# A new list of steps for the first stage and the first pair of a fused attention and FFN kernel

## Chip, cores and metric

The kernel runs on one core of one Trainium2 chip. The metric is the device time of one execution in microseconds, of which three runs of the kernel before are given, and one further execution was profiled.

## What is computed

Attention in two directions between x (8 batches, 8 heads, 512 rows, 64) and a state (32 rows), then two feed-forward layers over the 8 x 544 rows of 512 that come out of it:

```python
def _attn_ref(x, state):
    scores = scale * np.matmul(x, state.transpose(0, 1, 3, 2))
    ...
    xread = np.matmul(a, state)
    scores2 = scale * np.matmul(state, x.transpose(0, 1, 3, 2))
    ...
    sread = np.matmul(a2, x)
    return np.concatenate([xread, sread], axis=2)

def _moe_ref(x, w_in, w_out, g_ln):          # w_in 512x1024, w_out 1024x512
    h = x @ w_in
    ...                                      # solu = h * softmax(h), layer norm, times g_ln
    return ln @ w_out

def _moe2_ref(x, w_in, w_out):               # w_in 512x2048, w_out 2048x512
    h = x @ w_in
    g = np.maximum(0.01 * h, h)
    return g @ w_out
```

## The kernel before

The kernel has a first stage, a first pair of the second feed-forward layer, and three more pairs.

**The first stage** runs over eight batches b. Per batch it loads the state (`z`, in four pieces) and x (`xn`, in four pieces), transposes both on TensorE (tiles `zt`, `xt`), takes the scores (`st`), turns them and normalizes them on VectorE (`q`, `ee`), turns the two attention matrices (`a2t` on TensorE; `a1T` on VectorE by STREAM_TRANSPOSE), reads the state (`sr`) and forms state @ w_in (`sw` for the first batches, `sv` later, the latter from tiles `wi` loaded back from a DRAM copy `wsc`). The hidden rows `h` are a matmul of `a1T` with that product; they are normalized on VectorE and ScalarE (`sn`, `e`), turned (`tr` into `ln`) and multiplied by w_out (tiles `x2_b_r`, `x` in the profile), and the result leaves for a DRAM buffer (`xo` to `xs`). The weights arrive as 64-bit numbers (`raw_in`, `raw_out`) and are narrowed to f32 on ScalarE and VectorE first: for each quarter one Abs, two TENSOR_SCALAR and two SCALAR_TENSOR_TENSOR.

**The first pair** is the second feed-forward layer for the first two batches, in eight chunks of its width: the weights are narrowed and split, `hX`/`h` rows (`H`), the leaky step (`C`, `S`, `g`), and the second product (`o` added into `oacc`) which at the end goes out (`out<-oacc`, two transfers of 1 MB). With it run the rows of the states (`out8`, `oacc8`). **The later pairs** use a scheme with seven products (`hX`, `hY`, `hZ`, `oX`, `oY`, `oZ`), written in `rest()` from the lists PATTERN, HEAD and TURN. The first steps of the first later chunk are mixed into the tail of the first pair (tokens that begin with `/8.`).

**What sets the order.** Every operation is a generator that yields after each step. The string PROGRAM names generators; each occurrence of a name runs the next step of that generator:

```python
    for u in PROGRAM.split():
        if u not in stages:
            stages[u] = stage(u)
        if stages[u] is not None:
            next(stages[u], None)
```

The letters: `a` loads a quarter of w_in, `i` narrows it, `j` splits it into two parts, `b`, `o`, `p` the same for w_out; `z` and `x` load state and x of a batch, `Z` and `T` turn them, `S` is the scores, `U` the softmax, `A` and `B` turn the attention matrices, `R` reads the state, `Y` and `W` form state @ w_in, `w` loads a `wi` tile, `h` makes hidden rows, `t` turns them, `X` multiplies by w_out. `D`, `c`, `d`, `H`, `O`, `K`, `Q` are the first pair, `F` is `rest()`.

The class `InOrder` wraps every engine and the SP queue and ties each instruction to the one before it there, so each engine runs what the string says in that order and nothing is rescheduled. Because that helper records every instruction, all have the line L51 in the profile. Buffers are taken from rings when a step takes one and go back when the last user drops it (`take`, `drop`):

```python
    def take(ring, name, uses=1):
        held[name] = [ring, free[ring].pop(0), uses]
        return f"{ring}{held[name][1]}"
```

so the string also decides which buffer each tile lives in and whose release it waits for. All transfers are issued by the SP queue, one after the other.

Of the kernel before, what the change touches and what calls it, by code (L numbers as in the profile page):

```python
# [64 lines left out]
def attn_solu_leaky_kernel(  # L65
# [1291 lines left out]
    a0 i0 i0 i0 i0 i0 z0. Z0.1 a1 x0.0 T0.0 Z0.0 a3 i1 i1 i1 Z0.0 Z0.0 z1. i1 T0.0 i1 T0.1 T0.1  # L1357
    a2 S0.0 x0.1 i3 Z0.1 Z1.1 i2 Z1.1 Z0.1 T0.3 Z1.1 T0.2 Y0.0.0 i3 i3 i3 T0.3 z2. i2 i2 i2 T0.2
    i2 Z1.0 S0.1 Y0.0.0 S0.0 S0.0 Z1.0 Z1.0 j2 j2 b0 i3 S0.1 S0.1 o0 U0.0 U0.1 S0.0 b2 b3 o2
    Y0.0.1 S0.0 U0.0 U0.1 S0.1 S0.1 Y0.1.0 S0.1 S0.0 Y0.0.1 Y1.0.0 U0.1 U0.1 Y0.1.1 U0.1 U0.0  # L1360
    U0.0 U0.0 A0.1 b1 g Y1.0.0 A0.0 Y0.1.0 j3 Y1.1.1 o2 o2 A0.0 A0.1 R0 j2 Y1.1.1 Y0.1.1 B0.0 o0
    o1 Z2.0 B0.1 o1 Y1.1.0 R0 Z2.0 x1 o1 o0 o1 h0.1 Z2.0 Z2.0 h0.1 Y1.1.0 R0 h0.0 o1 o1 o0 R0
    Z2.0 h0.1 Y1.0.1 h0.1 Y1.0.1 o2 T1.0 h0.0 o0 T1.0 h0.1 h0.1 z3. T1.1 T1.1 h0.0 Z2.1 o2 S1.0
    h0.0 T1.2 T1.3 T1.2 S1.0 S1.0 T1.3 h0.0 h0.0 S1.0 S1.1 S1.0 S1.1 S1.1 h0.1 h0.0 U1.1 h0.2
    S1.1 h0.0 o0 h0.3 S1.0 U1.1 Z2.1 U1.0 U1.1 h0.0 h0.3 S1.1 h0.1 S1.1 U1.0 U1.0 h0.1 A1.0 A1.0
    A1.1 A1.1 h0.0 j1 t0.0.0 t0.0.0 U1.1 U1.1 h0.2 h0.1 t0.1.0 h0.3 t0.0.1 U1.0 U1.0 t0.1.0 h0.3
    h0.2 h0.3 j3 t0.0.1 R1 R1 B1.0 Z3.0 B1.1 h0.3 h0.2 h0.2 t0.1.1 h0.2 t0.1.1 h1.2 x2. R1 h0.3
    h0.3 h0.3 Z2.1 Z3.0 Z3.0 h1.2 h0.2 h1.0 R1 h0.3 t0.3.1 Z3.0 Z2.1 Z2.1 Z3.0 h0.2 t0.3.0 T2.2
# [60 lines left out]
    h6.1 h7.1 t6.1.0 t6.2.0 t6.2.0 h7.1 h7.0 t6.3.0 X5.1 X5.3 t6.2.1 h7.1 t6.3.1 h7.0 t6.1.0
# [93 lines left out]
```

## Time and profile before

| | |
|---|---|
| time, three runs | 1155.01, 1156.82, 1158.55 us (median 1156.82) |
| the profiled execution | 1156.16 us, span 1154.4 us |
| instructions | 16468 |
| matmuls | 6192 records, TensorE busy 98% of the span |
| VectorE, ScalarE, GpSimd | busy 78%, 47%, 47% |

In the profile's rows PE is TensorE, PEld its weight loads, DVE VectorE, ACT ScalarE, POOL GpSimd, SP (or SPq) the queue that issues the transfers. An instruction is named by the tile it writes and those it reads, so `xt<-ident,xn` turns a piece of x. Square brackets behind a row hold the idle time of the engine before it and what it waited for. Times are microseconds from the start of the span.

### The profile page before, as it was taken

What the parts mean: (1) busy time and instruction counts of PE and PEld (TensorE: products, weight loads), DVE (VectorE), ACT (ScalarE), POOL (GpSimd) and SP (SyncE); (2) the same over time, 40 slices, a digit from 0 to 9 for tenths busy, and PEclk for the clock granted to TensorE, in tenths of its full rate; (3) what the DMA queues carried; (4) which work ended last, traced back from release to release, by engine and by line L of the source; (5) the groups of instructions that cost most, each with busy time, mean ns of one, the idle gap of its engine ahead of it and who ended that gap; (6) DMA issues with size and microseconds to landing.
All of it is one profiled execution on the core that took longest, in us unless ns stands there. A gap on an engine that the chain in (4) does not pass through costs nothing.

```text
span 1154.4 us, 16468 instructions
## 1 busy us (share of the span) xinstructions
PE 1128.9 (98%) x6192; PEld 945.8 (82%) x6192; DVE 895.7 (78%) x1406; ACT 540.7 (47%) x907; POOL 540.2 (47%) x411
## 2 busy tenths in 40 slices
PE   6999999999999999999999998999999999999997
PEld 2565887888888888888887888998898998899997
DVE  7997868786887678468777977788977868877787
ACT  5676746655655554644343343334442324433231
POOL 2142420111202133756757458878656656745453
PEclk9999999999999999999999999999999999999999
DMA  9333222503523344763755585766877476655342
GB/s 317 93 107 136 55 96 64 139 19 92 152 70 108 130 162 155 246 210 131 243 208 202 183 346 220 289 238 229 318 292 273 179 278 254 236 222 236 148 192 74
DMA packets 88376, 211.85 MB, mean 184 GB/s; under 512 B 41320, under 2 KB 49512, under 8 KB 79080
## 3 DMA queue, kind: packets, MB, share of 16 engines
q1 hardware_dynamic: 88296, 210.79, 51.7%
q8 instruction: 49, 0.80, 0.3%
q14 instruction: 31, 0.25, 0.1%
HBM read 151.00 MB, written 59.77 MB: 183 GB/s over the span
## 4 chain that ended last, share of the span: by engine, by line
PE 89%; DMA 4%; DVE 3%; issue 1%; POOL 1%; ACT 0%; POOLq 0%; SPq 0%; DVEq 0%; ACTq 0%
PE x L51 17%; PE hX L51 14%; PE oX L51 10%; PE h L51 10%; PE o L51 8%; PE hY L51 7%; PE oY L51 5%; PE hZ L51 3%; PE tr L51 3%; PE sr L51 2%; PE oZ L51 2%; PE st L51 2%; PE sv L51 1%; DVE C L51 1%; PE sw L51 1%
## 5 line engine op out<-in xcount | busy, mean ns | idle before, releaser
L51 DVE TENSOR_TENSOR oacc<-oacc,oX 128x512 f32<-128x512 f32 x171 | 116.2, 683 | 52.9 <-PE oX L51 51.0
L51 PE MATMUL x<-ln,w_out_hi 128*128 128x512 f32 (+1 forms) x512 | 153.8, 384 | 0.0
L51 PE MATMUL hX<-xbT,w 128*128 128x512 f32 x576 | 149.9, 395 | 1.5 <-ACT C L51 1.2
L51 ACT COPY C<-hX 128x512 f32<-128x512 f32 x96 | 56.4, 587 | 171.1 <-PE hX L51 171.0
L51 PEld LDWEIGHTS hX<-xbT,w 128*128 128x128 f32 x576 | 103.4, 188 | 21.3 <-ACT C L51 1.6
L51 PEld LDWEIGHTS x<-ln,w_out_hi 128*128 128x128 f32 x512 | 92.2, 188 | 17.6
L51 PE MATMUL h<-sw,a1T 128*128 128x512 f32 x352 | 103.6, 436 | 0.0
L51 PE MATMUL x<-ln,w_out_lo 128*128 128x512 f32 (+1 forms) x256 | 97.2, 380 | 0.0
L51 POOL TENSOR_TENSOR gc<-C,gc 128x512 fp32r<-128x512 f32 (+1 forms) x43 | 69.3, 1614 | 50.2 <-ACT gc L51 25.5
L51 POOL TENSOR_TENSOR gb<-C,gb 128x512 fp32r<-128x512 f32 (+1 forms) x43 | 69.8, 1629 | 45.9 <-ACT gb L51 23.6
L51 DVE SCALAR_TENSOR_TENSOR C<-C 128x512 f32<-128x512 f32 (+1 forms) x88 | 82.7, 940 | 0.6
L51 PEld LDWEIGHTS h<-sw,a1T 128*128 128x128 f32 x352 | 64.1, 188 | 23.2 <-issue 11.0
L51 DVE TENSOR_TENSOR C<-C,hY 128x512 f32<-128x512 f32 x64 | 43.9, 686 | 43.7 <-ACT C L51 35.2
L51 DVE TENSOR_TENSOR oacc<-oacc,oY 128x512 f32<-128x512 f32 x93 | 63.3, 683 | 2.7 <-PE oY L51 2.0
L51 DVE TENSOR_TENSOR oacc<-oacc,o 128x512 f32<-128x512 f32 x70 | 45.7, 681 | 21.6 <-PE o L51 21.3
L51 PEld LDWEIGHTS x<-ln,w_out_lo 128*128 128x128 f32 x256 | 48.1, 188 | 9.8
L51 DVE TENSOR_TENSOR ln<-tr,ln 128x512 fp32r<-128x512 f32 x60 | 40.4, 684 | 17.9 <-ACT ln L51 17.5
L51 POOL TENSOR_TENSOR gb<-S,gb 128x512 fp32r<-128x512 f32 x27 | 44.6, 1656 | 16.8 <-ACT gb L51 8.1
L51 ACT CAST ln<-tr 128x512 fp32r<-128x512 f32 x60 | 34.5, 588 | 35.3 <-PE tr L51 35.2
L51 PE MATMUL hX<-xbB,w 128*128 128x512 f32 x192 | 50.9, 401 | 0.0
L51 POOL TENSOR_TENSOR gc<-S,gc 128x512 fp32r<-128x512 f32 x26 | 39.3, 1521 | 24.6 <-ACT gc L51 12.7
L51 PE MATMUL hY<-xbB,w 128*128 128x512 f32 x192 | 49.7, 394 | 0.4 <-DVE C L51 0.4
(696 smaller groups left out, 2801.8 us busy)
## 6 DMA issues: line engine op xcount, KB each, us to landing
w<-w2s SPq DMA_DIRECT2D x24, 1792.0 KB, 11.6
shared<-wo2s SPq DMA_DIRECT2D x24, 768.0 KB, 4.3
wi<-wsc SPq DMA_DIRECT2D x14, 1024.0 KB, 5.7
xs<-xo SPq DMA_DIRECT2D x34, 256.0 KB, 2.4
raw<-in_moe_w_in SPq DMA_DIRECT2D x8, 1024.0 KB, 5.6
raw<-in_moe_w_out SPq DMA_DIRECT2D x8, 1024.0 KB, 6.3
w2s<-w SPq DMA_DIRECT2D x8, 1024.0 KB, 8.1
wo<-wt2s SPq DMA_DIRECT2D x8, 1024.0 KB, 6.3
```

The costliest lines, as they stand in the source:

```text
L51: done = call(*args, **kw)
```

## The change

The string PROGRAM is written anew: 142 lines become 143, and nearly every token stands elsewhere. No instruction is added, removed or changed; the last token `F`, and so the three later pairs, is the same. What differs is the order on each engine up to the end of the first pair, the order of the transfers on SP up to there, and which buffers the tiles take. The first two lines of the list, the place of the load of x for batch 4, and the last two lines:

```diff
-    a0 i0 i0 i0 i0 i0 z0. Z0.1 a1 x0.0 T0.0 Z0.0 a3 i1 i1 i1 Z0.0 Z0.0 z1. i1 T0.0 i1 T0.1 T0.1
-    a2 S0.0 x0.1 i3 Z0.1 Z1.1 i2 Z1.1 Z0.1 T0.3 Z1.1 T0.2 Y0.0.0 i3 i3 i3 T0.3 z2. i2 i2 i2 T0.2
...
-    Z5.0 R3 t2.3.0 t2.3.1 h3.0 t2.0.0 x4. Z5.0 Z5.0 t2.3.1 t2.3.1 h3.0 t2.0.1 t2.0.0 t2.3.0
...
-    /8.t3 /8.t2 /8.hS3 /8.hS2 Q7.1 O0.7.1.1 /8.gA12 /8.t4 /8.hS4 O0.7.1.3 /8.gS3 /8.gS2 O0.7.1.1
-    O0.7.1.3 /8.ub /8.uc /8.gS1 /8.gS4 /8.gA22 Q7.1 F
+    a0 i0 i0 i0 a1 x0.0 T0.0 z0. i1 T0.0 T0.1 Z0.0 Z0.0 i0 a3 i0 a2 Z0.1 z1. T0.1 i1 i1 Z0.1 i1
+    Z0.1 i1 Z0.0 i3 i3 S0.0 i3 S0.0 i2 S0.0 Y0.0.1 x0.1 Y0.0.1 b0 S0.0 b2 i2 i3 i2 Z1.0 Z1.0
...
+    h2.3 h2.3 h2.3 w2.0 h2.3 t2.0.0 X1.3 X1.2 X1.3 t2.0.0 Z5.0 Z5.0 h3.0 h3.0 Z5.0 t2.3.0 t2.3.0
+    x4. T4.0 T4.0 T4.2 T4.1 h3.3 h3.3 h3.0 t2.3.0 T4.2 T4.2 h3.0 T4.1 T4.0 t2.2.0 h3.0 t2.2.0
...
+    O0.7.1.2 /8.t4 /8.hS2 /8.gS2 /8.hS4 O0.7.1.1 O0.7.1.1 /8.gS1 O0.7.1.3 /8.ub /8.uc /8.gS3
+    /8.gS4 F
```

Three places at which the order moves:

VectorE, about 32 to 42 us, where the first batch's a1T is made (`ee` is the attention matrix, `wo` and `w_out_f` the quarters of w_out, `sm` the softmax sums). Before:

```order
L51 TENSOR_REDUCE sm0_0_295<-ee0_256 128x16
L51 TENSOR_SCALAR sm0_0_295<-sm0_0_295 128x16
L51 RECIPROCAL sm0_0_295<-sm0_0_295 128x16
L51 TENSOR_SCALAR wo2_264<-wo2_264 128x1024 x2
L51 STREAM_TRANSPOSE a1T1_335<-ee0_256 128x512
L51 TENSOR_SCALAR wo0_254<-wo0_254 128x1024
L51 STREAM_TRANSPOSE a1T1_335<-ee0_256 128x512
L51 TENSOR_SCALAR wo1_338<-wo1_338 128x1024 x2
L51 TENSOR_SCALAR wo0_254<-wo0_254 128x1024
L51 SCALAR_TENSOR_TENSOR wo1_338<-raw_out0_246,wo1_338 128x1024
L51 TENSOR_TENSOR stq_87<-zt2_0_340,stq_87 128x64
```

Now:

```order
L51 RECIPROCAL sm0_0_313<-sm0_0_313 128x16
L51 TENSOR_SCALAR wo1_308<-wo1_308 128x1024
L51 TENSOR_REDUCE sm0_1_341<-ee0_272 128x16
L51 TENSOR_SCALAR sm0_1_341<-sm0_1_341 128x16
L51 RECIPROCAL sm0_1_341<-sm0_1_341 128x16
L51 TENSOR_SCALAR wo1_308<-wo1_308 128x1024
L51 TENSOR_TENSOR stq_87<-zt2_1_306,stq_87 128x64
L51 STREAM_TRANSPOSE a1T1_352<-ee0_272 128x512
L51 COPY srT_89<-sr0_318 64x4x32
L51 TENSOR_TENSOR stq_87<-zt2_1_306,stq_87 128x64
L51 SCALAR_TENSOR_TENSOR wo0_250<-raw_out0_211,wo0_250 128x1024
L51 STREAM_TRANSPOSE a1T1_352<-ee0_272 128x512
```

Both halves of `a1T1` now stand behind more of the narrowing of w_out: its last half has three further TENSOR_SCALAR and one SCALAR_TENSOR_TENSOR of `wo` ahead of it. Up to the a1T of the second batch both lists hold the very same instructions of VectorE.

SP, where x of batch 4 is loaded (`wi2_0`, `wi2_1` are 1 MB tiles of split w_in, `xs` are results on their way to DRAM). Before:

```order
L51 DMA xs1_67<-xo1_2_1349 128x512
L51 DMA wi2_0_1357<-wsc0_98 128x2048
L51 DMA wi2_1_1361<-wsc1_99 128x2048
L51 DMA xn_91<-in_x 128x8x64 x4
L51 DMA xs1_67<-xo1_3_1395 128x512
```

Now:

```order
L51 DMA z0_83<-in_state 32x2x64 x4
L51 DMA wi2_0_1400<-wsc0_98 128x2048
L51 DMA xs1_67<-xo1_2_1301 128x512
L51 DMA xn_91<-in_x 128x8x64 x4
L51 DMA wi2_1_1517<-wsc1_99 128x2048
L51 DMA xs1_67<-xo1_3_1411 128x512
```

The load of `wi2_1` moves from just ahead of the four pieces of `xn` to just behind them; a load of the state comes to stand ahead of `wi2_0`.

SP at the end of the first pair (`out` the results, `wf2` the first of the f32 weights that the later pairs take differences of, `wt2s`, `shared` the second product's weights). Before:

```order
L51 DMA w2_1_1_5488<-w2s1_103 128x3584
L51 DMA out_0<-oacc_3932 128x2048
L51 DMA out_0<-oacc8_4157 4x32x512
L51 DMA wt2s0_130<-wo2_1_0_5349 128x2048
L51 DMA shared_5350<-wo2s1_111 128x1536
L51 DMA out_0<-oacc_3932 128x2048
L51 DMA wt2s1_131<-misc_3964 128x2048
L51 DMA out_0<-oacc8_4157 4x32x512
L51 DMA wf2_5596<-wf2s2_120 128x1024
L51 DMA w2_1_2_5613<-w2s2_104 128x3584
```

Now:

```order
L51 DMA w2_1_1_5471<-w2s1_103 128x3584
L51 DMA shared_5351<-wo2s1_111 128x1536
L51 DMA wt2s0_130<-wo2_1_0_5350 128x2048
L51 DMA out_0<-oacc8_4202 4x32x512 x2
L51 DMA out_0<-oacc_3934 128x2048 x2
L51 DMA wt2s1_131<-misc_3930 128x2048
L51 DMA wf2_5596<-wf2s2_120 128x1024
L51 DMA w2_1_2_5613<-w2s2_104 128x3584
```

The two transfers of `oacc`, of 1 MB each, now stand side by side ahead of `wt2s1` and `wf2`, where before the first of them stood at the front; `shared`, `wt2s0` and both `oacc8` now go ahead of them.

## Rows read from the trace of the kernel before

**Rows 1.** Page, part 1: the span, and each engine's busy time, share and instructions.

```profile
span 1154.4 us, 16468 instructions
PE 1128.9 (98%) x6192; PEld 945.8 (82%) x6192; DVE 895.7 (78%) x1406; ACT 540.7 (47%) x907; POOL 540.2 (47%) x411
```

**Rows 2.** TensorE's waits, whole span: us in total, times, longest.

```profile
PE zt L51 <- DMA z<-in_state: 6.9, 1, 6.9
PE xt L51 <- DMA xn<-in_x: 5.3, 5, 2.3
```

**Rows 3.** Busy time by stretch, 0 to 66 us (stretch, its length, busy times).

```profile
0.00:20.00 20.00, 9.29 (x24) 4.49 (x25) 12.14 (x14) 8.36 (x15) 3.87 (x11) 1.00 0.94 276
...
sum 66.00, PE 55.04 PEld 31.28 DVE 56.95 ACT 40.53 POOL 15.73; mean PE 18.35 PEld 10.43 DVE 18.98 ACT 13.51 POOL 5.24
```

**Rows 4.** Busy time by stretches of 50 us: PE first, GB/s last.

```profile
150.00:200.00 50.00, 48.07 (x259) 40.16 (x258) 36.65 (x78) 27.18 (x56) 8.30 (x14) 1.00 0.30 90
200.00:250.00 50.00, 50.00 (x263) 41.93 (x262) 41.43 (x79) 30.83 (x58) 6.92 (x11) 1.00 0.32 88
...
650.00:700.00 50.00, 46.90 (x258) 40.66 (x257) 39.58 (x48) 22.75 (x36) 26.65 (x19) 1.00 0.65 246
```

**Rows 5.** Timeline of TensorE, first 66 us: start, us, operation, [idle before].

```profile
6.92 0.44 PE L51 MATMUL zt<-ident,z 128*128 128x128 f32 x1 [6.92 <-DMA z<-in_state]
9.63 1.99 PE L51 MATMUL xt<-ident,xn 128*128 128x128 f32 x4 [2.27 <-DMA xn<-in_x]
...
29.99 1.04 PE L51 MATMUL a2t<-ident,q 128*128 128x128 f32 x8
...
65.65 1.88 PE L51 MATMUL h<-sw,a1T 128*128 128x512 f32 x4
```

**Rows 6.** Timeline of VectorE, first 66 us.

```profile
7.17 1.42 DVE L51 TENSOR_SCALAR wi<-wi 128x1024 f32<-128x1024 f32 x2 [7.17 <-ACT wi L51]
8.63 1.23 DVE L51 SCALAR_TENSOR_TENSOR wi<-raw_in,wi 128x1024 uint32<-128x1024 uint32 x1
...
64.45 1.30 DVE L51 STREAM_TRANSPOSE a1T<-ee 128x512 f32<-128x512 f32 x2
```

**Rows 7.** Timeline of SP, 165 to 182 us (the duration is that of issuing).

```profile
165.68 0.92 SPq L51 DMA_DIRECT2D wi<-wsc  x2
168.84 7.42 SPq L51 DMA_DIRECT2D xn<-in_x  x4
```

**Rows 8.** Timeline of TensorE at the same place.

```profile
181.15 1.20 PE L51 MATMUL xt<-ident,xn 128*128 128x128 f32 x9 [1.93 <-DMA xn<-in_x]
```

**Rows 9.** Page, part 6: transfers, KB each, median us from issue to landing.

```profile
wi<-wsc SPq DMA_DIRECT2D x14, 1024.0 KB, 5.7
```

**Rows 10.** Timeline of TensorE, 302 to 305 us.

```profile
302.24 1.89 PE L51 MATMUL sr<-ee,xn 128*128 128x64 f32 x16
303.94 0.94 PE L51 MATMUL sv<-wi,stq 128*128 128x512 f32 x3
304.73 1.89 PE L51 MATMUL sr<-ee,xn 128*128 128x64 f32 x16
```

**Rows 11.** The chain that ended last, two of its pieces: start, us, what.

```profile
211.85 4.10 PE x L51 x18
...
306.62 4.19 PE x L51 x18
```

**Rows 12.** Timeline of SP at the end of the first pair.

```profile
678.20 0.34 SPq L51 DMA_DIRECT2D out<-oacc  x1
...
681.78 0.84 SPq L51 DMA_DIRECT2D wf<-wf2s  x1
```

**Rows 13.** Timeline of GpSimd there.

```profile
693.14 0.74 POOL L51 TENSOR_TENSOR wd<-wf 128x256 f32<-128x256 f32 x1 [8.55 <-DMA wf<-wf2s]
```

**Rows 14.** Timeline of TensorE there.

```profile
699.03 0.84 PE L51 MATMUL oX<-shared,gc 128*128 128x256 f32 x4 [3.10 <-POOL gc L51]
```

**Rows 15.** Busy time there, with clock, DMA share and GB/s at the end.

```profile
676.00:695.00 19.00, 19.00 (x123) 17.18 (x122) 12.09 (x16) 9.93 (x18) 10.06 (x8) 1.00 0.97 371
```

More of the change, by code (lines that the diff above doesn't have):

```diff
@@ new lines @@
+    h1.3 o3 h1.1 h1.1 U2.1 U2.1 h1.3 S2.1 p3 o2 S2.1 U2.0 j1 h1.2 W1.0.0 W1.0.1 h1.2 W1.0.0
+    W1.0.1 W1.0.0 W1.0.1 W1.0.0 W1.0.1 h1.0 X0.1 X0.1 h1.0 U2.0 U2.0 W1.1.0 U2.1 W1.1.0 X0.2
+    w1.3 W1.3.1 X0.2 X0.2 U2.0 X0.2 p2 U2.1 W1.3.1 U2.0 S2.0 W1.3.1 h1.0 h1.0 h1.2 h1.2 h1.2
+    h1.3 h1.3 W1.3.1 X0.1 B2.0 X0.1 X0.2 j1 W1.1.0 W1.1.0 X0.0 X0.0 h1.0 t1.0.0 S2.1 X0.0 X0.2
+    h1.3 W1.3.1 B2.0 t1.0.0 B2.0 h1.1 W1.1.0 p0 A2.1 X0.0 A2.1 W1.3.0 h1.3 t1.0.0 X0.0 A2.0
+    t1.0.1 U2.1 B2.1 A2.0 W1.3.0 h1.3 X0.3 h1.1 W1.1.1 X0.3 t1.0.1 t1.0.1 X0.0 X0.3 h1.1 W1.1.1
@@ new lines @@
+    h4.2 h4.2 B5.1 X3.3 B5.1 Z7.0 B5.1 h4.3 h4.3 Z7.0 Z7.0 Z7.0 X3.2 Z7.0 h4.3 X3.3 X3.3 X3.3
+    t4.1.1 h4.2 h4.2 h4.2 X3.2 B5.0 t4.1.1 t4.1.1 B5.0 B5.0 T6.0 R5 X3.2 T6.3 T6.0 T6.0 T6.1
+    T6.3 T6.3 t4.1.0 T6.1 T6.1 h5.0 X3.3 X3.2 t4.1.0 t4.1.0 h5.0 T6.2 h5.0 T6.2 T6.2 t4.3.0
+    t4.3.0 t4.3.1 t4.2.0 h5.1 t4.3.0 h5.0 X3.2 t4.2.1 t4.3.1 h5.0 t4.2.0 h5.0 S6.0 t4.2.0 h5.0
+    S6.0 t4.3.1 S6.0 h5.1 X4.2 S6.1 U6.0 S6.0 h5.1 t4.2.1 Z7.1 S6.0 S6.0 h5.0 t4.2.1 h5.0 h5.0
+    S6.1 S6.1 h5.2 h5.2 S6.1 U6.1 U6.1 X4.2 X4.2 h5.1 h5.1 Z7.1 h5.1 h5.2 w3.1 U6.1 t5.0.0
@@ new lines @@
+    X4.3 B6.0 x7. W3.2.0 W3.3.0 X4.3 W3.3.1 W3.3.0 W3.3.1 W3.2.1 X4.3 W3.2.1 W3.3.1 h6.0 t5.2.0
+    h5.1 t5.2.1 W3.2.1 W3.2.1 t5.2.0 t5.2.0 t5.1.1 h6.0 h6.0 h6.3 t5.2.1 t5.2.1 h6.3 W3.2.1
+    t5.1.0 t5.1.1 t5.1.1 T7.0 h6.0 h6.0 t5.3.0 t5.3.0 T7.1 h6.3 h6.2 T7.1 t5.3.0 h6.2 T7.1
+    t5.1.0 t5.3.1 h6.0 T7.3 t5.1.0 T7.0 T7.0 X5.2 h6.3 h6.3 T7.3 T7.2 X5.2 t5.3.1 t5.3.1 T7.2
+    h6.2 T7.2 S7.0 X5.2 S7.0 S7.0 h6.0 h6.0 T7.3 h6.2 h6.3 S7.1 h6.3 U7.0 S7.1 h6.0 X5.0 X5.0
+    X5.0 X5.0 U7.1 S7.0 h6.2 h6.1 h6.3 h6.2 U7.0 U7.0 h6.0 U7.1 U7.1 S7.1 S7.1 h6.2 S7.0 X4.3
@@ new lines @@
+    d4.0.0 d2.1.2 Q1.1 Q1.1 K2 d4.0.0 d3.0.3 d3.0.3 O0.1.0.2 O0.1.0.2 d4.0.0 H0.2.6 d4.0.0
+    O0.1.0.0 d4.0.1 d4.0.3 d4.0.3 H0.3.1 H0.3.2 H0.3.2 d4.0.3 d4.0.3 H0.2.7 Q1.0 K2 H0.2.6 Q1.0
+    H0.3.3 H0.3.4 O0.1.0.3 O0.1.0.3 H0.2.6 d2.1.1 O0.1.1.0 H0.3.4 H0.3.4 O0.1.1.1 d4.0.2 H0.2.5
+    H0.3.5 O0.0.1.1 O0.1.1.0 d2.1.4 K2 O0.1.1.3 K2 d4.0.2 K3 d5.0.0 H0.3.6 H0.3.1 O0.1.0.0
+    d5.0.0 K3 H0.3.5 H0.3.5 H0.4.0 H0.4.1 d5.0.0 d3.1.0 H0.2.5 d5.0.0 O0.1.1.3 d4.0.3 d4.0.3
+    O0.1.1.2 H0.4.0 H0.4.2 K2 H0.3.6 H0.4.2 O0.2.1.1 d3.0.5 K3 d3.1.0 d3.1.0 H0.3.7 H0.3.5
@@ new lines @@
+    Q3.0 d5.1.0 d4.0.5 H0.5.2 K4 H0.4.7 K4 H0.5.3 d6.0.0 d6.0.0 H0.5.2 H0.5.4 H0.5.4 H0.4.5
+    O0.3.0.1 H0.4.6 d5.1.0 O0.3.0.2 d4.1.2 Q4.1 d5.0.4 d6.0.0 O0.3.1.3 O0.3.0.2 Q3.0 H0.4.5
+    d5.1.0 d6.0.3 H0.5.1 d6.0.2 d6.0.3 d6.0.3 K5 O0.3.1.1 d6.0.2 K5 H0.5.4 H0.5.5 O0.3.0.0
+    H0.5.6 d5.1.0 d5.1.1 d6.0.1 H0.4.6 d5.1.5 O0.4.0.2 d5.0.5 O0.3.1.1 O0.3.0.3 K5 H0.5.5 d6.0.3
+    H0.5.5 O0.4.0.2 d6.0.4 H0.6.0 Q4.1 O0.3.1.2 H0.5.7 O0.3.0.3 O0.3.1.2 d6.0.3 d4.1.4 H0.5.6
+    H0.6.0 H0.5.6 d6.0.3 O0.3.1.0 d5.1.2 H0.6.1 H0.6.2 O0.4.0.3 H0.6.1 H0.6.2 O0.3.1.0 d5.1.2
@@ new lines @@
+    Q5.0 d7.1.0 Q5.0 H0.6.6 H0.6.6 H0.6.5 Q5.1 H0.7.2 H0.7.3 K6 Q5.1 /7.U O0.5.0.2 /7.ua K6
+    d7.1.0 d7.1.0 O0.5.1.3 H0.7.2 H0.7.4 /7.W H0.7.4 H0.7.4 O0.5.0.1 K6 H0.6.5 Q6.0 d7.1.0
+    H0.7.5 H0.7.6 L1.1 Q6.0 O0.5.0.0 H0.7.6 O0.6.0.3 H0.7.7 O0.6.0.3 O0.5.1.1 H0.7.6 d7.1.2
+    d7.1.2 O0.6.1.2 O0.5.1.1 O0.6.1.2 H0.7.5 H0.7.5 O0.5.0.2 O0.6.1.1 d6.1.4 H0.7.5 O0.6.1.1
+    H0.7.5 O0.6.0.2 O0.6.0.1 O0.6.0.2 O0.6.1.0 d7.1.5 O0.6.0.0 O0.5.0.1 k1.1 O0.6.0.1 k1.0 Q6.1
+    O0.6.1.3 /7.V l1 f1.0 k1.0 k1.6 f1.1 d7.0.4 d7.0.5 k1.3 k1.3 O0.6.1.0 f1.3 k1.1 k1.2 /8.m0
```

224 lines of the change are left out of this document (94 added, 130 removed).

## The prediction

> **What bounds the kernel now.** The page's first part comes first: TensorE is busy 1128.9 of 1154.4 us, and no other engine gets beyond 82% [rows 1]. So no step can win more than the 25.5 us in which TensorE stands still, unless its matmuls themselves come closer together. The change ends before about 700 us, so the next question is how much of that idle time lies ahead of it. The table of busy time by stretches answers: 10.71 us in the first 20 us [rows 3], 1.93 between 150 and 200, nothing between 200 and 250 (and so in the other stretches up to 600, within 0.3), 3.10 between 650 and 700 [rows 4]. Some 16 us in all are open to the new list, two thirds of them at the start.
>
> What these are is told by TensorE's waits and its timeline. The first matmul waits 6.92 us for the first load, which no order of steps makes arrive much earlier, since something must be loaded first [rows 2, 5]. Waits for x cost 5.3 us [rows 2]: 2.27 at 9.63 us [rows 5], 1.93 at 181.15 us [rows 8], and the 1.1 left over between them at the start (5.3 - 2.27 - 1.93). The 3.10 us at 699 us are a wait for GpSimd [rows 14].
>
> One more limit does not show in TensorE's own rows. VectorE starts at 7.17 us [rows 6] and is busy 56.95 of the 58.83 us from there to 66.00 [rows 3]. The hidden rows of the second batch, at 65.65 us, start as the last a1T transposes end, at 64.45 + 1.30 us [rows 5, 6]. So up to 66 us VectorE is as much the bound as TensorE; behind that TensorE alone.
>
> **The change part by part.** Nothing is added, so the cost of each part is a wait that goes or comes.
>
> *Start: taken as 0.* The list loads both halves of the first w_in tile first, then x, then the state, and puts two groups of `sw` matmuls ahead of the second half of x. The same bytes are queued in a stretch where the transfers are busy 0.94 of the time [rows 3], so the first products can't come much earlier or later. The two groups can fill the 1.1 us for which TensorE waits for x. What decides is what becomes of it: the second batch's a1T has the very same VectorE instructions ahead of it in both orders (the order's first place shows them swapped, not added), and VectorE had 58.83 - 56.95 = 1.9 us of idle time to lose or give. A lead that TensorE wins before is lost in waiting for that a1T at about 65.7 us. The first batch's a1T comes later than before, by three TENSOR_SCALAR (half of 1.42 each) and one 1.23 us SCALAR_TENSOR_TENSOR [rows 6], 3.4 us, and TensorE waits for it in the hidden rows; but that wait too lies ahead of the same 65.7 us. Ends: -1.1 (the wait for x goes, and VectorE closes as much of its idle time) and +1.9 (VectorE loses as much again as it stood idle before). I take 0, because VectorE's own work is the same and hardly any of its idle time can go.
>
> *x of batch 4: -1.9.* Before, two loads of `wi` (1 MB each) are issued at 165.68 us, right ahead of the four pieces of x, whose issuing then takes 7.42 us [rows 7]; TensorE stands 1.93 us for the last [rows 8]. Now one of the two goes behind x. At the 371 GB/s that the transfers reach when they are saturated [rows 15], 1 MB is 2.8 us, more than the wait. The state's load that now stands ahead is 16 KB a piece by its shape. So the wait goes. Ends: -1.93, and -1.0 if the queue ahead is otherwise fuller.
>
> *A load of wi at about 300 us: +0.4.* In the new list the last `wi` tile of round 3 (`wi3_2`) takes the buffer that `sv3_0_0` frees, and its first use `sv3_2_0` stands behind 16 `sr` matmuls, 3 `sv` and 12 `x` matmuls. From start to start these take 1.70 and 0.79 us [rows 10] and 12 x 0.23 = 2.75 us [rows 11], 5.2 us in all; such a load takes 5.7 us in the median [rows 9]. The rest, 0.5 us, is less where the queue is empty, as it is around 300 us; I take 0.4. Ends: 0, and 1.5 if the store of `xs` (256 KB by its shape) ahead of it on SP is still in flight. The Trainium skill (DMA: Bandwidth & Descriptors, section Bandwidth) lists 6.15 us for a load of 1 MB; by that the term would be 0.9 and the sum 0.5 us higher. The trace's own 5.7 stands here.
>
> *End of the first pair: 0.* Before, `wf` is issued at 681.78 us [rows 12] into a queue that moves 371 GB/s at a share of 0.97 [rows 15]; GpSimd, in order, stands 8.55 us for it until 693.14 us [rows 13] with the `gc` behind it for which TensorE then waits 3.10 us [rows 14]. Now the first `out` (1 MB) is issued beside the second, at about 678 us [rows 12] instead of at the front of this stretch, so 2.8 us of transfer are added right ahead of `wf`; `shared` (0.75 MB by its shape) and one `out<-oacc8` (0.25 MB) go ahead earlier by as much, 2.8 us. The last step of the pair and so the last `out` stays where it is in TensorE's work. These cancel. Ends: -3.1 (the wait is gone) and +2.8 (the 1 MB without what goes ahead).
>
> Everything between has buffers and loads as long ahead as before, as far as the order shows; TensorE is without a gap there [rows 4] and I count 0 for it. Sum: 0 - 1.9 + 0.4 + 0 = -1.5 us against the profiled execution's own 1156.16 us, 1154.7 us. That execution is 0.66 us below the median of the three runs; against the median of 1156.82 the forecast is **1155.3 us**. Its own range is 1153.4 to 1158.5: the terms' nearer ends (start -0.5 to +1.0, x -1.0 to -1.9, wi 0 to 1, end of the pair -1 to +1) and a little more for the runs, which are 3.5 us apart themselves. A measurement of this kernel tells about 0.3%, 3.5 us, from no change, so the forecast is a change that can't be told.
>
> **The rivals.**
>
> *Faster: the waits go.* The start keeps the 1.1 us, x of batch 4 gives 1.9, and the wait for `gc` at 699 us goes wholly (3.1), because `shared` and the small outputs leave the queue early enough that `wf` lands 3 us sooner. 1156.8 - 6.1 = 1150.7 us. For it: all three are waits for transfers, and the list touches the order of all three. Against it: VectorE's limit at 65.7 us, and 1 MB more just ahead of `wf`.
>
> *Slower: the outputs side by side.* The two `out` transfers wait for the pair's last sums, and SP runs in order, so `wt2s1` and `wf` stand behind them now. If VectorE's last sums come 3 us later than before, everything behind them on SP is issued so much later, and 1 MB more lies in the queue (2.8 us): `wf` lands up to 5.8 us later, GpSimd's `wd` and `gc` with it, and the wait of 3.1 becomes 8.9. With the -1.5 of the other terms, 1156.8 - 1.5 + 5.8 = 1161.1 us. It decides from the point at which `wf` lands 1.5 us later than before (no gain left) and is told from no change from 5 us on. For it: GpSimd already stands 8.55 us for this transfer [rows 13], so every microsecond goes through. Against it: 1 MB leaves the stretch as well.
>
> *Slower: VectorE at the start.* If VectorE waits for a load or for TensorE's scores in the first 66 us, each microsecond passes to the end; it had only 1.9 us of idle time. With 5 us of it: 1160.3 us. For it: more of w_out's narrowing stands ahead of the a1T. Against it: the same work, and a start of VectorE that hangs on the same first load.
>
> *The matmuls' own distance.* Two pieces of the chain with the same 18 matmuls take 4.10 and 4.19 us [rows 11], so the distance from matmul to matmul isn't quite constant: 2%. TensorE's rows show no gap for it. A list that gives tiles other buffers could shift a part: 500 matmuls of the touched part, each nearer or farther by those 0.09 / 18 = 0.005 us, are 2.5 us, up or down, within what can't be told. The Trainium skill (Perfetto Trace Analysis, its opening note) calls the busy time of matmuls a bad metric, because they are pipelined, and would read the 82% of the weight loads instead; by that far more than 16 us could be open to an order. No row of before bears it out beyond those 2%, so it gets a small chance.
>
> **How the numbers follow.** The forecast 0.54; faster by the waits 0.20; the outputs 0.14; VectorE at the start 0.06; the matmuls' distance 0.06, half up and half down and mostly within 0.3%. That gives faster by over 0.3% (below 1153.3) 0.23, with a part of the forecast's low edge; within it 0.55; slower (above 1160.3) 0.22. The range of eight in ten takes in the faster rival's 1150.7 and the slower one's 1161.1: 1150.5 to 1161.5.
>
> **What the profile after would show.** Start: TensorE's hidden rows of the second batch at 65.2 to 66.5 us, right behind a1T. If they come at 64 the start gains, at 68 VectorE was the bound. Batch 4: no wait for xn near 180 us, and 5.3 us of such waits down to 3.4 or less. At 300 us: a wait of `sv` for `wi` of up to 1 us. End of the pair: `wf` landing 11 to 12 us after its issue, and a wait of `oX` for `gc` of 2 to 4 us. I am wrong if a wait of more than 2 us shows between 66 and 650 us, if the wait for `gc` is gone or doubled, or if the same matmuls take longer without a gap.

## The result, and the profile after

The new list takes 1145.01 us in the median of four runs (1144.2 to 1146.07), beside 1157.62 us for the one before (four runs, 1155.01 to 1158.55): a ratio of 0.9895, 95% interval 0.9876 to 0.9915, some 12 us or 1% less. The forecast was 1155.3 with a range from 1150.5; the time lies below it. The profiled execution of the new list took 1145.32 us.

Its page, part 1 [rows 1 before], and TensorE's waits [rows 2 before]:

```profile
span 1143.5 us, 16477 instructions
PE 1124.3 (98%) x6192; PEld 944.0 (83%) x6192; DVE 894.3 (78%) x1406; ACT 539.6 (47%) x907; POOL 540.8 (47%) x411
```

```profile
PE xt L51 <- DMA xn<-in_x: 9.0, 1, 9.0
PE zt L51 <- DMA z<-in_state: 1.5, 1, 1.5
...
PE oX L51 <- POOL gc L51: 0.3, 1, 0.3
```

Before, the line of the wait for `gc` was

```profile
PE oX L51 <- POOL gc L51: 3.4, 2, 3.1
```

The wait for x is now the first one of the program (x is turned before the state) and the only one. The wait for `gc` is down from 3.4 to 0.3. And TensorE is busy 4.6 us less, though its matmuls are the same. The stretches of [rows 4] tell where TensorE has no gap any more:

```profile
150.00:200.00 50.00, 50.00 (x269) 42.05 (x267) 39.09 (x82) 27.79 (x54) 11.42 (x17) 1.00 0.31 90
...
650.00:700.00 50.00, 50.00 (x281) 43.56 (x280) 38.90 (x51) 23.41 (x38) 32.05 (x24) 1.00 0.74 288
```

Since the order differs, equal times aren't equal work. The table counts the matmuls instead: at each place, the start time of a matmul less the sum of the usual distances of all matmuls ahead of it (0.231 us for 512 columns in one pass, 0.429 for 512 columns of plain f32, 0.119 for 256, 0.112 for 64, 0.109 for a piece of a transpose, all medians of the trace). What is left is time in which TensorE stood, was held between two matmuls without a gap that the rows show, or ran slower.

| stretch (by work) | before | new list | difference |
|---|---|---|---|
| start to 70 us | 16.45 | 14.91 | -1.5 |
| 70 to 160 | 0.33 | 0.30 | 0.0 |
| 160 to 200 (x of batch 4) | 2.18 | 0.26 | -1.9 |
| 200 to 620 | 0.66 | 1.04 | +0.4 |
| 620 to 680 | 1.17 | -0.22 | -1.4 |
| 680 to 720 (wait for `gc`) | 4.91 | -0.04 | -5.0 |
| 720 to the end, same order | 5.87 | 4.47 | -1.4 |

The largest part is one that was forecast as 0. It is more than the wait itself, and the timeline of before tells why. TensorE behind the wait of [rows 14], and the stretch with its granted clock:

```profile
699.67 2.76 PE L51 MATMUL hX<-xbB,w 128*128 128x512 f32 x6
```

```profile
695.00:700.00 5.00, 1.90 (x13) 1.69 (x13) 3.44 (x4) 1.95 (x4) 5.00 (x5) 0.95 0.71 270
```

Six `hX` matmuls take 2.76 us there, and 1.55 in the new list. After the gap the granted clock fell to its lower level (1.2 GHz), and each of these six was 0.43 us from the next instead of 0.23: 1.2 us. With the matmuls around them the lower clock costs 1.6 us on top of the 3.3 that the wait takes from start to start, 4.9 in all. The Trainium skill (TensorE: Matmul & The Clock Gate, section HAM oscillation — how this bites in real kernels) has it that a wait for data between matmuls can throttle the clock again, so that the next ones start cold. The trace agrees here, with 1.6 us behind a gap of 3.1.

It does not happen every time. Of the seven profiles of this document that have this wait (2.9 to 3.6 us), the clock fell behind it in five, and the stretch costs 4.8 to 5.3 us by the count; in start_only and fill_only it stayed up behind waits of 3.2 and 2.9 us, and the stretch costs 3.4 and 3.2. The shorter waits at the start and for x of batch 4 are followed by it in a part of the profiles too (below).

The new list at the same place, SP, GpSimd and TensorE in turn [rows 12 to 14 before]:

```profile
663.18 0.32 SPq L51 DMA_DIRECT2D wt2s<-wo  x1
665.61 7.75 SPq L51 DMA_DIRECT2D out<-oacc  x4
675.14 0.33 SPq L51 DMA_DIRECT2D wt2s<-misc  x1
675.52 1.19 SPq L51 DMA_DIRECT2D wf<-wf2s  x1
```

```profile
683.86 0.74 POOL L51 TENSOR_TENSOR wd<-wf 128x256 f32<-128x256 f32 x1 [6.35 <-DMA wf<-wf2s]
```

```profile
691.03 0.88 PE L51 MATMUL oX<-shared,gc 128*128 128x256 f32 x6
691.75 1.55 PE L51 MATMUL hX<-xbB,w 128*128 128x512 f32 x6
```

`wf` lands 8.3 us after its issue, 3 us less than before (681.78 to 693.14), and it is issued 1.9 us earlier in TensorE's work: 4.0 us behind the first `oX` of the later pairs instead of 5.9. While `wf` is under way the transfers move 403 GB/s over 11.3 us in the kernel before, 4.6 MB, and 388 GB/s over 8.4 us in the new list, 3.3 MB.

The start, TensorE and VectorE [rows 5, 6 before]:

```profile
8.99 2.98 PE L51 MATMUL xt<-ident,xn 128*128 128x128 f32 x8 [8.99 <-DMA xn<-in_x]
...
14.96 1.88 PE L51 MATMUL sw<-sw,stp 128*128 128x512 f32 x4
18.38 0.30 PE L51 MATMUL zt<-ident,z 128*128 128x128 f32 x1 [1.54 <-DMA z<-in_state]
...
28.09 1.16 PE L51 MATMUL a2t<-ident,q 128*128 128x128 f32 x8
```

```profile
6.85 1.42 DVE L51 TENSOR_SCALAR wi<-wi 128x1024 f32<-128x1024 f32 x2 [6.85 <-ACT wi L51]
...
15.80 1.42 DVE L51 TENSOR_SCALAR wi<-wi 128x1024 f32<-128x1024 f32 x2 [1.15 <-ACT wi L51]
...
63.35 1.30 DVE L51 STREAM_TRANSPOSE a1T<-ee 128x512 f32<-128x512 f32 x2
```

TensorE starts 2.1 us later and is 1.9 ahead at its `a2t`. It stands as long as before in the first 20 us (10.9 us instead of 10.7); what the start wins are matmuls that follow each other sooner. The second batch's a1T comes 1.1 us earlier, though the same instructions of VectorE stand ahead of it and a new wait of 1.15 us lies in it. VectorE starts 0.3 us earlier and is at the a1T 56.5 us later instead of 57.3; of these it is idle 2.6 us instead of 1.8, so it is its work that got shorter. 1.1 us of that are two TENSOR_SCALAR that run beside GpSimd. Before, VectorE and GpSimd:

```profile
30.55 1.05 POOL L51 TENSOR_TENSOR ee<-ee,sm 128x512 f32<-128x512 f32 x1 [4.06 <-DVE sm L51]
30.95 0.68 DVE L51 TENSOR_SCALAR sm<-sm 128x16 f32<-128x16 f32 x1
31.83 2.08 DVE L51 TENSOR_SCALAR wo<-wo 128x1024 f32<-128x1024 f32 x2
32.06 1.30 POOL L51 TENSOR_TENSOR ee<-ee,sm 128x512 f32<-128x512 f32 x1 [0.46 <-DVE sm L51]
```

New list:

```profile
33.10 1.26 POOL L51 TENSOR_TENSOR ee<-ee,sm 128x512 f32<-128x512 f32 x1 [28.67 <-DVE sm L51]
34.08 0.31 DVE L51 TENSOR_SCALAR sm<-sm 128x16 f32<-128x16 f32 x1
```

The one of `sm` takes 0.68 us before and 0.31 now, and in both lists it ends 0.03 us after GpSimd's instruction; where it stands alone it takes 0.18 (at 29.91 us before). The second of the two `wo` takes 1.41 us before, and ends 0.5 us after GpSimd's second instruction; no `wo` takes over 0.69 in the new list. All nine profiles with VectorE's old order at the start have the 0.67 and the 1.41, all five with the new one have neither. No run moved these instructions alone.

### The profile page after: what moved, and what is told of

It reads as the page before. It is cut to its first block, busy times and chain, and to the rows that moved or that the text cites. A ratio compares the mean times of both kernels' runs of the same rounds, so it can differ in the third digit from the quotient of the medians.

```text
span 1143.5 us, 16477 instructions
## 1 busy us (share of the span) xinstructions
PE 1124.3 (98%) x6192; PEld 944.0 (83%) x6192; DVE 894.3 (78%) x1406; ACT 539.6 (47%) x907; POOL 540.8 (47%) x411
## 4 chain that ended last, share of the span: by engine, by line
PE 96%; DMA 1%; SPq 1%; DVE 1%; issue 0%; ACT 0%; POOLq 0%; DVEq 0%; POOL 0%
PE x L51 17%; PE hX L51 15%; PE oX L51 11%; PE h L51 10%; PE o L51 10%; PE hY L51 8%; PE oY L51 6%; PE hZ L51 4%; PE tr L51 3%; PE oZ L51 2%; PE sr L51 2%; PE st L51 2%; PE sv L51 1%; PE xt L51 1%; PE sw L51 1%; PE hs L51 1%
## 5 line engine op out<-in xcount | busy, mean ns | idle before, releaser
L51 DVE SCALAR_TENSOR_TENSOR C<-C 128x512 f32<-128x512 f32 (+1 forms) x88 | 79.9, 908 | 0.4
L51 POOL TENSOR_TENSOR ee<-ee,sm 128x512 f32<-128x512 f32 x16 | 17.5, 1098 | 92.0 <-DVE sm L51 92.0
L51 POOL TENSOR_TENSOR gb<-S,gb 128x512 fp32r<-128x512 f32 x27 | 43.4, 1614 | 17.1 <-ACT gb L51 10.9
```

The costliest lines, as they stand in the source:

```text
L51: done = call(*args, **kw)
```

## The experiments

All are lists of tokens like the two above. The kernel before was timed again beside each: its medians were 1156.05 us in the first four (x4_only, uc_early, start_only, end_only), 1155.40 in the next four (fill_only, tail_only, late_uc, z1_early) and 1158.73 in the last four, each four on another chip. So the ratios count more than the times; gains in us are worked out from them, and a ratio is not always that of the medians.

**x of batch 4 alone (x4_only).**

```diff
-    ... X1.2 w2.0 B3.0 B3.0 w2.1 h2.3 h2.3 ...
-    ... h3.0 t2.0.0 x4. Z5.0 Z5.0 ...
+    ... X1.2 w2.0 B3.0 B3.0 h2.3 h2.3 ...
+    ... h3.0 t2.0.0 x4. w2.1 Z5.0 Z5.0 ...
```

> The list of before with one token moved: the load of wi2_1 goes from just ahead of x of batch 4 to just behind it. Theory (each wait stands by itself): the 1.93 us wait of TensorE for xn near 181 us goes and the time is 1.9 to 2.1 us less, no other wait changes by more than 0.5 us. Rival (the queue stays full and only the name of the late transfer changes): TensorE still waits 1 us or more, for xn or later for wi2_1, and the time is within 1 us of before.

1154.44 us, ratio 0.9979 (0.9966 to 0.9992), 2.4 us less. TensorE has no gap left there:

```profile
175.00:190.00 15.00, 15.00 (x86) 12.71 (x85) 12.81 (x23) 10.14 (x21) 0.74 (x2) 1.00 0.57 145
```

By the count of the table the stretch costs 0.02 us instead of 2.18. This step of the prediction holds. In two of the other profiles (uc_early, tail_only) the clock fell behind this wait and the stretch costs 4.3 and 4.1 us, so the wait can be worth more than its length.

**The start alone, the end alone.** The first 445 tokens of the new list, then what the old one has left; and the old list's first 1784 tokens, then what the new one has left. Up to such places the two lists differ by a few tokens only.

```diff
-    (before) the old list
+    (start_only) the new list's tokens 1 to 445, then the old list without these
+    (end_only) the old list's tokens 1 to 1784, then the new list without these
+    (tail_only, below) the old list's tokens 1 to 2023, then the new list without these
```

> The new list for its first 445 steps (to about 113 us), then the old one without those steps. Theory: the start alone is worth 1.5 us, since VectorE starts 0.3 us earlier and loses 0.8 us less on its way to the second batch's a1T; the hidden rows of that batch start at 64.2 us instead of 65.65, the wait for xn at 181 us and the wait for gc at 699 us stay. Rival (the prediction's own step): what TensorE wins is given back at the a1T or just behind, and the time is within 0.5 us of before.

1153.79 us, ratio 0.9976 (0.9952 to 1.0000): 2.8 us, but hardly told from nothing. In the profile the start (to 70 us) costs 14.8 us by the count, as in the new list, and the hidden rows of the second batch start at 64.05 us; between 70 and 160 us it costs 1.8 instead of 0.3, most of it just behind the place where the two lists are joined: TensorE waits 0.6 and 0.3 us for VectorE near 132 and 134 us, which it does in neither list alone. So this run doesn't tell the theory from its rival: the start is worth 1.5 us up to 70 us, and the joint takes most of that back.

> The old list for its first 1784 steps (to about 585 us), then the new one without those steps. Theory: the waits of 0.5 and 0.6 us near 635 and 641 us, the wait for gc with the clock's fall behind it (4.6 to 5.0 us) and 1 to 1.5 us of waits in the unchanged list behind 700 us go with this part, 7 to 8 us in all, two thirds of the whole gain. Rival (the gain is spread, by buffers and the distance of matmuls all over): the end alone gives 3 to 5 us and nothing behind 720 us.

1148.54 us, ratio 0.9924 (0.9900 to 0.9948): 8.8 us, most of the whole. By the count it loses 0.06 us between 680 and 720, and 5.1 behind 720, hardly less than before's 5.9. So the gain lies ahead of 720 us, and the part of the theory that counted on the unchanged list behind it is not borne out: over the profiles of all these kernels that stretch costs anything from 2.6 to 5.9 us. The profile loses 0.05 us between 620 and 660 us, where before had 1.3. With x4_only's 2.4 and start_only's 2.8 the three parts come to 14 us, the whole's 12 within their intervals.

**What frees the queue at the end of the pair.** First `wt2s0` (with the step of VectorE that makes it, token `/7.uc`) and the load of `shared` (`/8.V`) were moved a little way up:

```diff
-    /8.gA11 /8.m5 O0.7.0.0 O0.7.1.0 /8.l11 /8.hA22 O0.7.1.2 O0.7.0.3 ... Q7.0 /8.ua Q7.0 /7.uc /8.V
+    /8.gA11 /8.m5 O0.7.0.0 O0.7.1.0 /8.l11 /8.hA22 O0.7.1.2 /7.uc /8.V O0.7.0.3 ... Q7.0 /8.ua Q7.0
```

> The list of before with two tokens moved up at the end of the first pair: wt2s0 (1 MB) and the load of shared (0.75 MB) are issued ahead of the first out instead of behind it and behind out8; TensorE's order is as before. Theory (what lies in the queue ahead of wf decides): wf lands 3 us sooner or more after its issue, so the wait of oX for gc near 699 us falls from 3.1 us to under 0.5, the six matmuls behind it take 1.5 instead of 2.8 us because the clock stays at its upper level, and the time is 4 to 5 us less. Rival (what decides is when SP issues wf, at 681.8 us, behind wt2s1): wf lands within 1 us of before, the wait stays at 2.5 us or more, the time within 1 us.

1156.68 us, ratio 0.9994 (0.9978 to 1.0011): nothing, as the rival had it. The profile (this execution ran 5 us later at this place):

```profile
675.00 0.32 SPq L51 DMA_DIRECT2D wt2s<-wo  x1
...
687.22 1.21 SPq L51 DMA_DIRECT2D wf<-wf2s  x1
```

```profile
698.34 0.74 POOL L51 TENSOR_TENSOR wd<-wf 128x256 f32<-128x256 f32 x1 [8.60 <-DMA wf<-wf2s]
```

11.1 us from issue to landing, hardly less than before's 11.4. The two had moved by only 3 us, and the first `out` behind them moved down: 386 GB/s over these 11.1 us are 4.3 MB, beside 4.6 before. The 5 us by which this execution ran later lie at two waits for x, behind which the clock fell, at 18 and at 185 us; in the profile of before it stayed up at both. So the two were moved as far as the new list has them (and away from their old place):

```diff
-    /8.e4 K7 K7 /8.W O0.7.1.2 k1.5 ...
+    /8.e4 K7 K7 /8.W /7.uc /8.V O0.7.1.2 k1.5 ...
```

> The list of before with two tokens moved some 10 us up at the end of the first pair, as far as the new list has them (uc_early had moved them by 3 us only): wt2s0 (1 MB) and the load of shared (0.75 MB) are issued near 664 us, into the stretch of 668 to 674 us in which the transfers rest; TensorE's order as before, wf issued in the same place. Theory (bytes still under way when wf is issued decide): wf lands 2.5 us sooner or more after its issue, the wait for gc falls from 3.1 us to 0.5 or less, the clock stays up behind it, and the time is 3 to 5 us less. Rival (the point at which SP issues wf, or the new list's whole end, is needed): the wait stays at 2 us or more, the time within 1.5 us.

1150.96 us, ratio 0.9938 (0.9917 to 0.9958), 7 us less (5 to 10) by two tokens.

```profile
664.86 0.32 SPq L51 DMA_DIRECT2D wt2s<-wo  x1
...
681.71 1.24 SPq L51 DMA_DIRECT2D wf<-wf2s  x1
```

```profile
690.49 0.73 POOL L51 TENSOR_TENSOR wd<-wf 128x256 f32<-128x256 f32 x1 [5.92 <-DMA wf<-wf2s]
```

```profile
695.00:700.00 5.00, 5.00 (x34) 4.58 (x34) 4.89 (x6) 2.58 (x5) 3.40 (x2) 1.00 0.53 192
```

`wf` is issued at the same time as before (681.78) and lands 2.6 us sooner after it; the gap and the fall of the clock are gone. Measured against TensorE's work, which is 0.8 us later here, `wf` is also issued 0.8 us earlier, so of the 3.4 us by which it lands sooner 2.6 are the queue. The stretch into which the two moved, before and in uc_far:

```profile
668.00:674.00 6.00, 6.00 (x28) 4.97 (x27) 5.89 (x9) 1.75 (x3) 5.21 (x5) 1.00 0.60 225
```

```profile
668.00:674.00 6.00, 6.00 (x28) 4.95 (x27) 5.22 (x8) 1.74 (x3) 4.92 (x6) 1.00 0.96 326
```

The expectation has the transfers at rest there; they were busy 0.60 of the time, and in uc_far 0.96. While `wf` is under way 349 GB/s over 8.8 us are moved, 3.1 MB instead of 4.6. By the count the wait's place (680 to 720 us) costs 0.1 us, 4.9 less than before. That the runs gain more than that goes with the clock in part: their mean granted clock is 0.9986, and 0.9957 in the runs of the kernel before beside them, a difference worth some 3 us by the line at the end of this section. And the other way round, in the new list, the two moved back behind the outputs:

```diff
-    ... /8.m5 /8.V /8.e5 ... /8.y6 /7.uc O0.7.0.2 ... O0.7.1.3 /8.ub /8.uc /8.gS3 /8.gS4 F
+    ... /8.m5 /8.e5 ... /8.y6 O0.7.0.2 ... O0.7.1.3 /7.uc /8.V /8.ub /8.uc /8.gS3 /8.gS4 F
```

> The new list with two tokens moved back at the end of the first pair: wt2s0 (1 MB) and the load of shared (0.75 MB) are issued behind both out transfers, right ahead of wt2s1 and wf, as late as before the change or later. Theory (the bytes that are issued in the last 15 us ahead of wf decide): wf lands 4 us later than with the new list, and TensorE waits 1.5 to 3 us for gc again; the time is 1.5 to 4 us more than the new list's 1145.0. Rival (what counts is that the two outs are issued late and together): wf lands within 1.5 us of the new list's, no wait for gc, time within 1 us of 1145.0.

1151.70 us, ratio to before 0.9965 (0.9952 to 0.9977), where the new list has 0.9895. TensorE, and the clock in two stretches:

```profile
695.35 0.97 PE L51 MATMUL oX<-shared,gc 128*128 128x256 f32 x4 [3.62 <-POOL gc L51]
696.12 2.76 PE L51 MATMUL hX<-xbB,w 128*128 128x512 f32 x6
```

```profile
690.00:695.00 5.00, 1.73 (x15) 1.53 (x13) 3.98 (x5) 2.75 (x5) 4.92 (x5) 1.00 0.97 372
695.00:700.00 5.00, 4.65 (x18) 4.02 (x19) 2.95 (x3) 1.08 (x3) 4.46 (x4) 0.66 1.05 424
```

The wait is back, and the fall with it. Here `wf` is also issued later, at 678.68 us, since VectorE splits `wt2s0` just ahead of `wt2s1`; of the 5.8 us by which it lands later, 3.2 are that and 2.7 the queue (11.0 us from issue to landing instead of 8.3). The time is 7 us over the new list's, more than the theory's 4; by the ratios it is 8, though the two were not timed side by side.

The last hundred tokens alone (tail_only, the old list's first 2023, then the new one's rest):

> The old list for its first 2023 steps (to about 640 us), the new one for the last hundred. Theory: the wait for gc goes with these alone, with the clock's fall behind it, 4 to 5 us less, and the 0.5 us wait near 635 us stays; the time is 5 to 7 us less, somewhat behind end_only. Rival (the transfers of the stretch 585 to 640 us, issued earlier in the new list, are what frees the queue): the wait for gc stays at 2 us or more and the gain is under 3 us.

1157.43 us, ratio 1.0009 (0.9994 to 1.0025): no gain. The wait for `gc` is gone (0.05 us by the count between 680 and 720), but another took its place, of `hX` for `xbB` from VectorE:

```profile
PE hX L51 <- DVE xbB L51: 3.0, 1, 3.0
```

Between 620 and 660 that costs 6.1 us by the count, where before had 1.3. Probably the new list's end counts on steps of VectorE that it does earlier, between 585 and 640 us; that wasn't tried. Neither theory had this: the wait for `gc` went as the first expected, the time did not.

**What carries the start.** One group of `sw` matmuls moved ahead of the second half of x in the old list; both groups moved back behind it in the new one; the order of the first loads alone; and in the new list the second load of the state moved up:

```diff
-    (old) Z1.1 Z0.1 T0.3 Z1.1 T0.2 Y0.0.0
+    (fill_only) Z1.1 Z0.1 Z1.1 Y0.0.0 T0.3 T0.2
-    (new) S0.0 Y0.0.1 x0.1 Y0.0.1 ... Y0.0.0 T0.2 Z1.1 Y0.0.0 T0.2 S0.0 i2 T0.3 Y1.0.1
+    (unfill) S0.0 x0.1 ... T0.2 Z1.1 T0.2 S0.0 i2 T0.3 Y0.0.1 Y0.0.1 Y0.0.0 Y0.0.0 Y1.0.1
-    (old) a0 i0 i0 i0 i0 i0 z0. Z0.1 a1 x0.0 T0.0
+    (sp_start) a0 a1 x0.0 i0 i0 i0 i0 i0 z0. Z0.1 T0.0
-    (new) T0.0 z0. i1 T0.0 T0.1 Z0.0 Z0.0 i0 a3 i0 a2 Z0.1 z1. T0.1
+    (z1_early) T0.0 z0. z1. i1 T0.0 T0.1 Z0.0 Z0.0 i0 a3 i0 a2 Z0.1 T0.1
```

> The list of before with one group of four sw matmuls moved ahead of the second half of x on TensorE, into the stretch of 16 to 19 us in which it waits for xn; transfers and VectorE in the old order. In two of five profiles so far in which that wait stands whole, the granted clock fell to 0.5 behind it for some 6 us, and the start was 3 to 3.5 us longer; with the new start it was at 1.00 in both. Theory (the gap and the clock's fall behind it are what the new start removes): the clock stays at 1.00 in the first 30 us, the wait falls by 1.7 us, and the time is 1.5 to 3.5 us less than before. Rival (the new order of the loads and of VectorE is what counts, since the a1T of the second batch comes no earlier): less than 0.7 us.

1153.77 us beside 1155.40, ratio 0.9994 (0.9980 to 1.0009): nothing that can be told. The clock stayed up at the start in the one profile, as the theory has it, and the a1T comes 0.3 us sooner. (Of the profiles with the old start up to then, four and not five, the clock fell in two.)

> The new list with the two groups of sw matmuls moved back behind the second half of x on TensorE, as they stood before the change. Theory (these groups are what carries the start): TensorE waits 2 to 3 us for xn before 20 us again, in some runs with the clock's fall behind it, and the time is 1.5 to 4 us more than the new list's 1145 to 1147. Rival (VectorE's and the loads' order carry it, TensorE has slack up to 64 us): within 1 us of the new list's.

1150.50 us, ratio to before 0.9934 (0.9917 to 0.9950). That is 4 to 5 us over the new list by ratio and by time, though not timed beside it. TensorE waits 2.4 us there, for z and not for x as expected, and 0.2 us for x. The clock after the gap, in this kernel and in the new list:

```profile
20.00:23.00 3.00, 3.00 (x9) 1.96 (x10) 2.97 (x7) 0.60 (x1) 0.00 (x0) 0.50 0.95 374
```

```profile
20.00:23.00 3.00, 3.00 (x15) 1.80 (x14) 2.97 (x7) 1.58 (x3) 0.00 (x0) 1.00 1.03 391
```

By the count the start (to 70 us) costs 19.2 us here, 14.9 in the new list. The second batch's a1T starts at 67.66 us instead of 63.35, although VectorE's order is the new one: VectorE waits 3.9 us for TensorE's scores at 29 us, which it does neither before nor in the new list. So the groups in the gap count because a late TensorE holds VectorE up.

> The list of before with the first loads in the new order (both halves of the first w_in tile, then x, then the state), all else as before. Theory (VectorE's start is worth 0.3 us and TensorE's wait at 17 to 19 us stays): within 1 us of before. Rival (the loads carry the start): 1.5 us less or more, with the a1T of the second batch a microsecond earlier.

1157.14 us, ratio 0.9991 (0.9973 to 1.0010): the loads alone do nothing, and the a1T comes at 66.0 us, 1.6 later than before. TensorE still turns the state first here, for which it now waits 11.6 us instead of 6.9; so this shows the loads without the order of TensorE that goes with them.

> The new list with one token moved: the second load of the state goes ahead of the second w_in tile instead of behind it, for which TensorE waits 1.5 us at 18.4 us in the new list. Theory: that wait goes, but TensorE then waits for the second half of x, and VectorE's way to the a1T at 63 to 64 us is the bound up to there, so the time is within 0.7 us of the new list's 1145.0. Rival (TensorE is the bound at the start): 1 to 1.5 us less, 1143.5 to 1144.

1146.77 us, ratio to before 0.9927 (0.9912 to 0.9942): no gain over the new list, but 1.8 us more by time and 3.7 by ratio (not timed beside it), where the theory had 0.7 at most. TensorE now waits 1.6 us at `xt`, for ScalarE and not for x; VectorE waits 3.2 us for the narrowed w_in, whose load now stands behind the state's, instead of 1.15. So the a1T comes at 65.25 us instead of 63.35, and the start costs 16.8 us by the count instead of 14.9: VectorE's way is the bound, as the theory has it, but the edit made it longer.

**Three places together (three_moves).** x4_only, uc_far and fill_only in one list, five tokens moved.

> The list of before with three places edited, five tokens in all: uc_far, x4_only and fill_only together. Theory (the waits stand by themselves, and each takes the clock's fall behind it along): 2.4 us of x4_only, 3 to 5 of uc_far and 0.5 to 2 of fill_only add up to 6 to 9 us less than before, 1147 to 1150 us, and the mean granted clock is 0.999 or more in most runs. Rival (a wait that is taken away comes back further on): less than 5 us.

1148.52 us (1147.98 to 1149.97), ratio 0.9920 (0.9904 to 0.9937), 9 us less: three quarters of the new list's gain. The waits add up, and the mean granted clock is 0.999 in all five runs.

**The clock over all runs.** Each run's mean granted clock is known. Over the 60 runs of the kernel before that were timed beside these lists, a line through them gives 1152.7 us plus 1.1 us for each 0.001 that the mean clock lies under 1 (the two runs at 1.000 took 1153.3 on average, the seven at 0.994 took 1160.4); on each of the three chips by itself it is 1.0 to 1.1. That is what the slow stretches themselves cost: 2.3 us at half the clock lower the mean of 1154 us by 0.001 and lose 1.15 us of work. The mean of the 60 is 0.9966, worth 3.8 us. All four runs of the new list have 1.000. So of the 12 us some 4 are matmuls at the lower clock, in places that differ from run to run, and the other 8 or so are waits. This division is an estimate from the line.

## Why the prediction was wrong

*What bounds the kernel* was read rightly, but the exception that it names came true. "No step can win more than the 25.5 us in which TensorE stands still, unless its matmuls themselves come closer together": they did, 4.6 us of the profile's 10.9 are busy time. A gap costs its length and, in some executions, what follows it at the lower clock. The row with the 2.76 us and the 0.95 was in the trace of before and entered no term.

*End of the first pair: 0.* This step failed; -5.0 in the profile, 7 to 9 us in the runs (uc_far, end_only). It has `wf` landing 11 to 12 us after its issue as before, because bytes ahead of it "cancel"; it lands after 8.3 us and the wait is gone. The sum set 1 MB of `out` against `shared` and a small output, 1 MB, and left out `wt2s0`, another 1 MB, although the order that was quoted shows it going ahead of the outputs as well. And it counted by the order on SP where the time counts: moved past one `out` (uc_early) the two transfers gain nothing, moved so far that they fill the stretch in which the transfers are busy only 0.60 of the time (uc_far) they take the wait away. That row was in the trace of before too. The step also priced the wait at 3.1 us, without the 1.6 us at the lower clock behind it. The rival that the waits go had the right mechanism (`wf` 3 us sooner), with 0.20, and was 6 us short, 1.6 of them this fall of the clock.

*Start: 0.* -1.5 in the profile, more than the far end of -1.1. The limit that was named, VectorE's way to the second batch's a1T, fits: in all five profiles with VectorE's new order TensorE starts on that batch 0.1 us after the first of the two a1T transposes has ended (64.16 us in the new list). But it came 1.1 us sooner. "VectorE's own work is the same" is where the step failed: the instructions are the same, and take 1.2 us less in sum, 1.1 of it in the two that run beside GpSimd; idle time did not go, it grew. In the runs the clock comes on top: of the seven profiles with the old order of TensorE at the start, four fell to half the clock behind the waits at 17 to 20 us, and of the four with the new one none. These waits don't decide it by their length: in sp_start 2.6 us were not followed by a fall. That the `sw` groups in the gap carry this is seen in unfill's one profile, where the clock falls and VectorE waits for TensorE; in the old list, fill_only gave too little to tell, and the fall showed again in three_moves. So how much of the start's gain is the clock's stays open.

*x of batch 4: -1.9.* Right, and for the reason given: -1.9 in the profile, and x4_only shows it by itself.

*A load of wi at about 300 us: +0.4.* No such wait shows; 0. The +0.4 of the table for 200 to 620 us is made of pieces of 0.2 us and less at other places.

*Everything between: 0.* 1.4 us too little: waits for VectorE near 635 and 641 us are gone (0.4 us idle each, 0.5 and 0.6 from start to start). The part behind 720 us came out 1.4 lower, within what the profiles differ there anyway. Why it differs stays open.

*The rivals that ended slower* had their places right and their sign wrong: with the outputs side by side `wf` lands 3 us sooner and not 5.8 later, and VectorE does wait at the start, 1.15 us for ScalarE's `wi`, but is at the a1T sooner all the same. The matmuls' own distance did not move: 0.231 us in both.

## What to carry to other kernels

Price a wait of the bounding TensorE by its length and by the slower matmuls behind it, and look for the granted clock in the stretch behind each gap, in more than one run. When a transfer is late, count the bytes still under way when it is issued: in this kernel moving two of them ahead helped only where they went into a stretch in which the transfers were not busy all the time. Two tokens did that here for 0.6% of the time, more than half of what the new list wins. And when an order is swapped on one engine, look at what its instructions now run beside on the others: the same instructions need not take the same time.

## What had not been expected of the hardware

The same kernel on one core scatters by 7 to 9 us over the 15 to 23 runs on one chip, and by 11 us over all 60 (1151.3 to 1162.2). Two thirds of the variance go with the granted clock: the same wait of about 2 us at the same place is followed by the lower level in some executions (behind 1.8 us at the start in uc_early, behind 2.3 us for x of batch 4 in tail_only) and not in others (2.6 us at the start in sp_start, 2.4 us for x of batch 4 in end_only). A list in which such waits are gone is faster by more than they are long. Its four runs lie within 1.9 us, the four of before beside them within 3.5; four are too few to call it steadier.

Two of VectorE's TENSOR_SCALAR take 0.68 us instead of 0.18 and 1.41 instead of 0.63 where GpSimd's TENSOR_TENSOR had started before them; one that started 0.2 us before GpSimd's (at 34.60 us in the new list) takes 0.63.
